# First hidden products in halves by head pair, tile 1's scores in one bank, another order of the first loads

## The chip, the core and the metric

The kernel runs on one core of a Trainium2 chip. The metric is the device time of one execution in microseconds (us); the kernel before takes 806.84 us (median of 3 runs, 805.37 to 808.19). The engines are PE (TensorE, matrix products; PEld is its weight load), ACT (ScalarE), DVE (VectorE), POOL (GpSimd) and SP (SyncE, which here only issues DMAs). Each runs its own instructions strictly in the order of its queue, and waits for the others by semaphores.

## The reference

Eight batches with eight heads of 576 tokens; the attention is local to chunks of 64 tokens, and its output (4608 tokens of 512 features) goes through a feed-forward block whose activation is h * cos(h).

```python
q_c, k_c, v_c = (a.reshape(B, H, S // 64, 64, D) for a in (q, k, v))
scores = (1.0 / np.sqrt(D)) * np.matmul(q_c, k_c.transpose(0, 1, 2, 4, 3))
scores = scores - np.max(scores, axis=-1, keepdims=True)
attn = np.exp(scores)
attn = attn / (np.sum(attn, axis=-1, keepdims=True) + 1e-09)
out = np.matmul(attn, v_c).reshape(B, H, S, D)
x = out.transpose(0, 2, 1, 3).reshape(B * S, H * D)       # 4608 x 512
h = x @ w_in                                              # w_in 512 x 2048
return (h * np.cos(h)) @ w_out                            # w_out 2048 x 512
```

The weights arrive as 64-bit floats, q, k and v as 32-bit ones.

## The kernel before

The 4608 tokens are nine tiles of 512. The work has two parts. In the first, tiles 0 and 1 (and the attention of tile 2) run while the weights arrive; each weight block (16 of `w_in`, 16 of `w_out`, 512 KB each) is turned from 64-bit bits into a float32 value and split into a high and a low part, so that a product of float32 accuracy is three fast matmuls: high by high, high by low, low by high (`hidden`, line 813; `split_weight`, line 504). In the second part the other tiles run in pairs with fewer products, from sums of weight blocks that the first part stored to HBM; its order is set by a planner of its own (`planned`), which the change does not touch.

The attention of tiles 0 and 1 (`early`, line 1138) goes by head pairs 0 to 3 (two heads side by side on the 128 partitions). For each pair: PE makes the scores (`scores_early`, 16 products of 64 x 64), DVE takes the maximum (L626) and subtracts it (L630), ACT exponentiates (L696), DVE sums (L712) and inverts (L716, L717), DVE or POOL multiplies by the inverse, called the quotient here (L481), PE transposes ("turns") the weights (L731), ACT copies them out (L477), PE multiplies by the values ("weighted"), and ACT and DVE split the result into the high and low part of x (L795, L798). Each pair's weighted result fills two PSUM banks, so four x splits make one half of x.

Weight blocks are read by two ACT instructions (`w`, L541, and `half`, L543), joined on DVE (L536), rounded to the high part on ACT or DVE (cast to `w_in` or `w_out`, L477 or L475), and the low part is the difference (L481 on POOL or DVE). `w` has two rooms, `half0` and `half1` one each.

A hidden block h(s) is 12 matmuls of 512 columns over the four pairs of x; the activation is six steps: ACT L831 rounds h/2pi, DVE L832 reduces, ACT L833 is the sine, which needs another function table than the exponential (so it comes behind all exponentials of tile 1), DVE L834 multiplies, which frees the PSUM bank of h, and the result is split (cast on ACT or DVE, `g_lo` on DVE or POOL). PSUM has eight banks: acc0 to acc3, two named h, and a0 and a1. h(0), h(1), h(3) and the later ones rotate over the two h banks; h(2) is in a1. So h(3) waits for L834 of h(0). The projection p(s), 12 matmuls of `g` and `w_out`, comes three hidden blocks later.

All of the first part is a list of pieces (`piece`, line 1046) with an engine, an assumed length and what each waits for. `placed` (line 162) puts them in an order by assumed times and by a due time from the table DUE, one number for each piece; `in_order` gives that order to the engines' queues. Pieces on PE that are longer than LONG go by due time, shorter ones as soon as they can.

Loads are issued by SP in one list. The first 22 issues (q and k of tile 0, `w_in` block 0, q and k of tile 1's pair 0, v of tile 0, `w_in` block 1, the other q and k of tile 1) come without a hold; behind them stand the remaining weight blocks. These are held by `touch` (line 1088), an instruction of one column on POOL that writes into the room of `w_in` block 2 and reads something that is ready late:

```python
raw, part = w_raw["in", 2][0].bitcast(F32)[:, :1], x_parts[0, 0][0][:, 0, :1].bitcast(F32)
two_by(POOL, raw, part, part, ALU.subtract)
```

Eight semaphores serve the loads in turn, so an issue also waits until the load eight places before it has landed.

Of the kernel before, what the change touches and what calls it, by code (L numbers as in the profile page):

```python
# [96 lines left out]
LONG = 2.0  # L97
# [33 lines left out]
    158.12, 58.9, 68.58, 63.65, 252.88, 143.8, 82.3, -250.55, 219.35, 114.51, -120.22, -295.86, 1e+09, -4.71,  # L131
# [5 lines left out]
    262.3, 48.25, 126.32, 193.62, 1e+09, 345.43, 23.97, -61.67, 75.14, -1.8, 433.58, 246.37, -62.79, 87.68, -8.61,  # L137
    -145.35, 32, 6.23, 84.32, 191.91, -66.13, 267.53, -107.91, 1e+09, 59.88, 1e+09, 1.78, 1e+09, 6.61, 1e+09,
    1e+09, -10.09, -254.05, 202.29, -15.1, 262.24, -166.36, 249.63, 71.08, 209.64, -226.64, 255.17, -18.33,
# [5 lines left out]
    -76.27, 1e+09, 292.24, -11.78, -101.18, 119.54, 173.07, 246.81, -59.42, 152.58, 59.6, 147.63, -111.18,  # L145
    -165.31, 170.18, 412.05, -234.16, 253.81, 56.94, 223.55, 174.74, 172.68, 262.87, 1e+09, -113.14, 133.26,
# [8 lines left out]
    199.71, 243.39, -154.74, 16.19, 1e+09, 1e+09, 143.88, -50.34, 1e+09, 1e+09, 1e+09, 1e+09, 1e+09, 1e+09,  # L155
    172.37, 92.61, 1e+09, 1e+09, 1e+09, 1e+09, 1e+09, 1e+09, 1e+09, 58.67, 248.55, 155.33, -25.97, 231.79, 141.91,
    1e+09, 1e+09, 153.74, 117.79, 119.81, 83.59, 470.08, 488.44, 258.14, 542.25, -17.83, 164.19, 314.55, 83.71,
    62.74, 350.71, -36.4, 242.13, -61.82, 228.28, 332.92, 1e+09, 437.5, 104.97, 27.99, 78.88, 1e+09, 458.39,
    -62.42, 304.54, 227.74, 1e+09, 424.55, 137.98, 50.14, 154.55, 190.64, 238.98, 240.92, 295.04, 313.65, -63.39,
    266.72, 327.78, 178.57, 212.45, 346.38, 151.22, 291.83, -2.81, 148.05, 154.34,  # L160
)


def placed(work, after_it, rank):

    n = len(work)
    left = [len(w[3]) for w in work]  # L170
# [266 lines left out]
def attention_then_cos_ffn(ctx: ExitStack, tc, qT, kT, v, w_in, w_out, out, wide):  # L437
# [630 lines left out]
    for hp in range(HP):  # L1068
        here["v", 0, hp] = loaded(0.25, load_v, 0, hp)
    here["in", 1] = loaded(0.5, load_weight, "in", 1)  # L1070
    for hp in range(1, HP):
        here["qk", 1, hp] = loaded(0.5, load_qk, 1, hp)
# [1386 lines left out]
```

## Time and profile before

| | us |
|---|---|
| median of 3 runs | 806.84 (805.37 to 808.19) |
| profiled execution, its own time | 804.86 |
| span of its instructions | 803.1 |
| PE busy | 789.8 (98%) |
| DVE, ACT, POOL busy | 691.7, 530.3, 204.0 |
| granted TensorE clock | 1.00 in all 40 slices |

The page's slices show PE busy at 9 tenths or more from the third slice on (a slice is 20 us), DVE likewise in most. Matmuls overlap one another, so a matmul's duration is longer than the step from one to the next; a row of 12 matmuls of one block takes about 2.72 us from its start to the start of what follows. Idle time in brackets is that of the engine just before the row, with what ended it.

### The profile page before, as it was taken

How to read it: one execution, taken by the hardware profiler on the slowest of the kernel's cores; microseconds unless marked ns; L12 is line 12 of the kernel's file. 1: busy time of each engine (PE TensorE's matmuls, PEld its weight loads, DVE VectorE, ACT ScalarE, POOL GpSimd, SP SyncE). 2: the span in 40 equal slices, each digit the busy share in tenths (PEclk: the TensorE clock that was granted, in tenths of full speed). 3: DMA queues.
4: the chain of work that ended last, by engine and by line, in shares of the span. 5: the costliest groups of instructions: out<-in, count | busy, mean ns of one | idle time of the engine just before them, and what ended most of it. 6: DMA issues, size and time to landing. Idle time of an engine off the chain costs nothing.

```text
span 803.1 us, 17487 instructions
## 1 busy us (share of the span) xinstructions
PE 789.8 (98%) x6720; PEld 698.8 (87%) x6720; DVE 691.7 (86%) x1071; ACT 530.3 (66%) x1006; POOL 204.0 (25%) x179
## 2 busy tenths in 40 slices
PE   5999999999999999999999999999999999999998
PEld 5788788888988898888999998888999988889998
DVE  6999998888888798999999988899999878789854
ACT  4988955455467766767777566889655566665552
POOL 2363765766812211410410001121001001000000
PEclk9999999999999999999999999999999999999999
DMA  8993739586988895987648779556665665556653
GB/s 315 388 417 140 263 131 317 182 309 200 281 301 245 315 311 197 305 285 245 205 154 268 236 222 323 204 196 199 222 215 185 194 222 189 183 184 211 211 184 105
DMA packets 95266, 189.88 MB, mean 236 GB/s; under 512 B 8656, under 2 KB 51664, under 8 KB 95184
## 3 DMA queue, kind: packets, MB, share of 16 engines
q1 hardware_dynamic: 95184, 188.78, 69.2%
q8 instruction: 53, 0.87, 0.4%
q14 instruction: 29, 0.24, 0.1%
HBM read 148.90 MB, written 39.85 MB: 235 GB/s over the span
## 4 chain that ended last, share of the span: by engine, by line
PE 90%; DMA 6%; DVE 2%; ACT 1%; issue 0%; SPq 0%; DVEq 0%
PE acc L471 55%; PE h L471 29%; PE a L471 5%; DMA w_out<-in_w_out_dram 5%; DMA kt<-in_kT_dram 1%; PE a L1585 1%; DMA qt<-in_qT_dram 1%; DVE w L536 1%; ACT g L833 0%; DVE g L832 0%; ACT w L541 0%; DVE w_in L481 0%; DVE g_lo L481 0%; DVE w_in L475 0%; DVE w_out L481 0%
## 5 line engine op out<-in xcount | busy, mean ns | idle before, releaser
L471 PE MATMUL h<-x,w_in 128*128 128x512 f32 (+1 forms) x852 | 190.6, 367 | 0.7 <-DVE g L834 0.7
L471 PEld LDWEIGHTS h<-x,w_in 128*128 128x128 f32 x852 | 147.8, 188 | 28.8 <-DVE g L834 1.4
L471 PE MATMUL acc<-w_in,w_in 128*128 128x512 f32 (+1 forms) x702 | 153.0, 346 | 0.0
L471 PEld LDWEIGHTS acc<-w_in,w_in 128*128 128x128 f32 x702 | 113.5, 188 | 16.6
L471 PE MATMUL acc<-w_out,g_hi 128*128 128x512 f32 x352 | 109.9, 393 | 0.3 <-DVE vt L475 0.3
L471 PE MATMUL acc<-w_in,g_hi 128*128 128x256 f32 x576 | 104.2, 282 | 0.0
L471 PEld LDWEIGHTS acc<-w_in,g_hi 128*128 128x128 f32 x576 | 88.3, 188 | 0.9
L471 PE MATMUL acc<-x,w_in 128*128 128x512 f32 x276 | 82.6, 392 | 0.0
L471 PE MATMUL acc<-w_in,g_lo 128*128 128x256 f32 x288 | 80.3, 279 | 0.0
L471 PEld LDWEIGHTS acc<-w_out,g_hi 128*128 128x128 f32 x352 | 64.2, 188 | 13.1 <-DVE vt L475 0.7
L471 PE MATMUL acc<-w_out,g_lo 128*128 128x512 f32 x176 | 68.7, 390 | 0.0
L1483 ACT ACTIVATE w_out<-w_out 128x512 f32<-128x512 f32 x96 | 60.1, 631 | 11.5 <-DVE w_out L1479 11.2
L481 DVE TENSOR_TENSOR g_lo<-w_out,g_hi 128x512 fp32r<-128x512 f32 x79 | 57.3, 730 | 10.8 <-ACT g_hi L477 9.1
L477 ACT CAST g_hi<-w_out 128x512 fp32r<-128x512 f32 x75 | 46.4, 620 | 28.2 <-PE acc L471 15.4
L471 PEld LDWEIGHTS acc<-x,w_in 128*128 128x128 f32 x276 | 51.6, 188 | 11.1
L471 PEld LDWEIGHTS acc<-w_in,g_lo 128*128 128x128 f32 x288 | 54.3, 189 | 0.0
L481 POOL TENSOR_TENSOR w_out<-g,w_out 128x512 f32<-128x512 f32 x10 | 14.2, 1422 | 143.1 <-ACT w_out L1483 143.1
L477 ACT CAST g_hi<-g 128x512 fp32r<-128x512 f32 x50 | 30.8, 623 | 25.6 <-DVE g L834 12.9
L481 POOL TENSOR_TENSOR g_lo<-w_out,g_hi 128x512 fp32r<-128x512 f32 x8 | 11.8, 1469 | 127.6 <-ACT g_hi L477 53.9
L471 PE MATMUL h<-w_in,g_hi 128*128 128x256 f32 x240 | 43.5, 282 | 0.0
L471 PEld LDWEIGHTS acc<-w_out,g_lo 128*128 128x128 f32 x176 | 33.0, 188 | 7.1
L1476 ACT ACTIVATE w_out<-g 128x512 int32<-128x512 f32 x48 | 29.9, 630 | 13.5 <-DVE g L1492 12.2
(216 smaller groups left out, 1687.0 us busy)
## 6 DMA issues: line engine op xcount, KB each, us to landing
w_in<-combo SPq DMA_DIRECT2D x112, 512.0 KB, 4.5
w_in<-sums SPq DMA_DIRECT2D x84, 512.0 KB, 3.5
combo<-w_in SPq DMA_DIRECT2D x56, 256.0 KB, 4.0
sums<-w_out SPq DMA_DIRECT2D x56, 256.0 KB, 4.5
qt<-in_qT_dram SPq DMA_DIRECT2D x36, 256.0 KB, 5.4
kt<-in_kT_dram SPq DMA_DIRECT2D x36, 256.0 KB, 5.4
w_in<-in_w_in_dram SPq DMA_DIRECT2D x16, 512.0 KB, 9.3
w_out<-in_w_out_dram SPq DMA_DIRECT2D x16, 512.0 KB, 9.9
```

Of the source, the lines that this page charges most:

```text
L471: kept(nc.tensor.matmul(*args, **kw))
L477: kept(nc.scalar.copy(out=out, in_=in_))
L481: kept(eng.tensor_tensor(out, a, b, op=op))
L536: kept(nc.vector.scalar_tensor_tensor(bits, bits, 3, low, op0=ALU.logical_shift_left, op1=ALU.bitwise_or))
L1476: kept(nc.scalar.activation(n.bitcast(I32), h, AF.Identity, bias=0.25, scale=0.5 / math.pi))
L1483: kept(nc.scalar.activation(g, g, AF.Sin, bias=0.5 * math.pi))
L1585: kept(nc.tensor.transpose(out=pt[:, i * P : (i + 1) * P], in_=e[:, 2 * i : 2 * i + 2].rearrange("p c k -> p (c k)"), identity=ident,))
```

## The change

The first two hidden blocks are made in halves: pairs 0 and 1 of h(0), then of h(1), then pairs 2 and 3 of both (HALVED, and `some` in `hidden`). LONG goes from 2.0 to 1.3, so that halves count as long pieces. Tile 1's scores all use bank a0, where they took a0 and a1 in turn; bank a1 takes the turned weights of tile 0's pairs 2 and 3, which used the two h banks. SP issues q and k of tile 1's pair 1 ahead of v of tile 0's pairs 2 and 3. `touch` reads tile 0's quotient of pair 3 (and waits for it), where it read the first x split. The assumed length of tile 1's weighted products is less, the assumed arrival of some loads later by 0.5, and the whole table DUE is another one (its rows are left out here).

```diff
-LONG = 2.0
+LONG = 1.3
+
+HALVED = 2
...
-        pt = ps_h.tile([P, 512], F32, name="h") if t == 0 else bank("a", hp)
+        pt = ps_h.tile([P, 512], F32, name="h") if t == 0 and hp < 2 else bank("a", hp if t else 1)
...
-    def hidden(t, fc):
-        h = bank("a", 1) if (t, fc) == order[2] else ps_h.tile([P, TOK], F32, name="h")
+    def hidden(t, fc, some=range(NCC), h=None):
+        if h is None:
+            h = bank("a", 1) if (t, fc) == order[2] else ps_h.tile([P, TOK], F32, name="h")
         w_hi, w_lo = w_parts["in", fc]
-        for cc in range(NCC):
+        for cc in some:
...
-    for hp in range(HP):
+    for hp in range(2):
+        here["v", 0, hp] = loaded(0.25, load_v, 0, hp)
+    arrival[0] += 0.5
+    here["qk", 1, 1] = loaded(0.5, load_qk, 1, 1)
+    for hp in range(2, HP):
         here["v", 0, hp] = loaded(0.25, load_v, 0, hp)
     here["in", 1] = loaded(0.5, load_weight, "in", 1)
-    for hp in range(1, HP):
+    arrival[0] += 0.5
+    for hp in range(2, HP):
         here["qk", 1, hp] = loaded(0.5, load_qk, 1, hp)
...
-        raw, part = w_raw["in", 2][0].bitcast(F32)[:, :1], x_parts[0, 0][0][:, 0, :1].bitcast(F32)
+        raw, part = w_raw["in", 2][0].bitcast(F32)[:, :1], weights_of(0, 1)[:, 1, 0, :1]
...
-            which = ("a", hp % 2) if t else ("acc", hp)
+            which = ("a", 0) if t else ("acc", hp)
...
+        if t == 0:
+            work[touch][3].append(q[3])
...
-            at = banks_free["a", hp % 2] if t else p.get(hp - 2)
+            at = banks_free["a", hp % 2] if t else banks_free.get(("a", 1)) if hp > 1 else None
...
+            elif hp > 1:
+                banks_free["a", 1] = banks_free["scored"] = p[hp]
...
-                PE, 0.9 * n if t else 0.8, made_by(key, lambda hps=hps, which=which: weighted(t, hps, [bank(*b) for b in which])),
+                PE, 0.6 * n if t else 0.8, made_by(key, lambda hps=hps, which=which: weighted(t, hps, [bank(*b) for b in which])),
...
-                if t == hp == i == 0:
-                    work[touch][3].append(hi)
...
+        if s < HALVED:
+            begun = piece(
+                PE, 1.36, made_by(("begun", s), hidden, t, fc, range(2)), begun, split["in", fc],
+                *x_done[t][:4], turned_out[0, 0],
+            )
+
+            def go(s=s, t=t, fc=fc, key=key):
+                made[key] = hidden(t, fc, range(2, NCC), made["begun", s])
+            stream = piece(PE, 1.36, go, stream, begun, *x_done[t])
```

What this does to the queues is seen at three places. On PE, from tile 1's second scores to the first hidden blocks, in the kernel before (`a0`, `a1` with `kt,qt` are scores of tile 1, `ident` marks a turn of tile 0's pairs 2 and 3, `x0` with `w_in0` is h(0)):

```order
L471 MATMUL a1_403<-kt_213,qt_212 64x64 x16
L731 MATMUL h_427<-ident_84,e1_282 128x128 x4
L731 MATMUL h_436<-ident_84,e1_282 128x128 x4
L471 MATMUL a0_483<-kt_217,qt_216 64x64 x16
...
L471 MATMUL a1_550<-kt_221,qt_220 64x64 x16
L471 MATMUL h_578<-x0_373,w_in0_441 128x512
...
L471 MATMUL h_578<-x0_524,w_in0_441 128x512
...
L471 MATMUL h_603<-x0_373,w_in1_591 128x512
```

The same stretch of PE now:

```order
L480 MATMUL a0_401<-kt_209,qt_208 64x64 x16
L740 MATMUL a1_464<-ident_84,e1_282 128x128 x4
L740 MATMUL a1_478<-ident_84,e1_282 128x128 x4
L480 MATMUL a0_487<-kt_217,qt_216 64x64 x16
...
L480 MATMUL a0_559<-kt_221,qt_220 64x64 x16
L480 MATMUL h_582<-x0_375,w_in0_508 128x512
...
L480 MATMUL h_596<-x0_375,w_in1_483 128x512
...
L480 MATMUL h_582<-x0_530,w_in0_508 128x512
```

The pieces stand in the same order; the banks differ, and the halves of h(0) and h(1) alternate behind tile 1's last scores.

On DVE, from the last inversion of tile 0 to tile 1's third subtraction, in the kernel before (L630 subtracts, L626 is the maximum, L481 the quotient, L536 joins a weight block, `w_308` being `w_in` block 0 and `w_380` block 1):

```order
L717 RECIPROCAL z_285<-z_285 128x16
L481 TENSOR_TENSOR e1_282<-e1_282,z_285 128x512
L630 TENSOR_TENSOR e0_332<-a0_315,m_333 128x512
...
L536 SCALAR_TENSOR_TENSOR w_308<-w_308,half0_89 128x512
...
L626 TENSOR_REDUCE m_420<-a1_403 128x8
L630 TENSOR_TENSOR e0_332<-a1_403,m_420 128x512
L626 TENSOR_REDUCE m_501<-a0_483 128x8
L536 SCALAR_TENSOR_TENSOR w_380<-w_380,half1_90 128x512
```

DVE there now (L639 subtracts, L635 is the maximum, L490 the quotient, L545 joins, `w_470` being block 1, L807 an x split, L721 a sum):

```order
L726 RECIPROCAL z_284<-z_284 128x16
L639 TENSOR_TENSOR e0_332<-a0_315,m_333 128x512
L490 TENSOR_TENSOR e1_282<-e1_282,z_284 128x512
...
L635 TENSOR_REDUCE m_418<-a0_401 128x8
L545 SCALAR_TENSOR_TENSOR w_470<-w_470,half1_90 128x512
L639 TENSOR_TENSOR e0_332<-a0_401,m_418 128x512
L545 SCALAR_TENSOR_TENSOR w_308<-w_308,half0_89 128x512
L807 TENSOR_TENSOR x0_376<-acc1_358,x0_375 128x4x64
L721 TENSOR_REDUCE z_510<-e0_332 128x8
L635 TENSOR_REDUCE m_505<-a0_487 128x8
L639 TENSOR_TENSOR e1_504<-a0_487,m_505 128x512
```

The subtraction of tile 1's pair 0 went ahead of the quotient, and both joins went between tile 1's second maximum and its third.

On ACT, from the last x splits of tile 0 to the first sine, in the kernel before (L543 and L541 read weight blocks, `w_in2_95`, `w_in3_97` and so on being blocks as they land, L795 an x split, L696 an exponential, L831 the first step of h(0)):

```order
L795 CAST x0_524<-acc2_529 128x4x64
L541 ACTIVATE w_572<-w_in2_95 128x512
L543 ACTIVATE half0_89<-w_in2_95 128x512
L477 CAST w_in1_591<-w_380 128x512
L543 ACTIVATE half1_90<-w_in3_97 128x512
L543 ACTIVATE half0_89<-w_out0_92 128x512
L696 ACTIVATE e1_500<-e1_500 128x512
L541 ACTIVATE w_601<-w_in3_97 128x512
L831 ACTIVATE g_618<-h_578 128x512
L696 ACTIVATE e1_500<-e1_500 128x512
L541 ACTIVATE w_626<-w_out0_92 128x512
L833 ACT_TABLE_LOAD
```

ACT there now (lines 9 or 10 higher):

```order
L552 ACTIVATE half1_90<-w_in3_97 128x512
L804 CAST x0_530<-acc2_536 128x4x64
L550 ACTIVATE w_579<-w_in2_95 128x512
...
L705 ACTIVATE e1_504<-e1_504 128x512
L552 ACTIVATE half0_89<-w_out0_92 128x512
L804 CAST x0_530<-acc3_537 128x4x64
L486 CAST w_in3_607<-w_589 128x512
L552 ACTIVATE half1_90<-w_in4_99 128x512
L550 ACTIVATE w_619<-w_out0_92 128x512
L841 ACTIVATE g_628<-h_582 128x512
...
L843 ACT_TABLE_LOAD
```

Two x splits of tile 0's pair 3 now stand behind the first reading of `w_in` block 3, and the first step of h(0) behind that of block 4, which in the kernel before came behind h(0)'s sine.

## Rows read from the trace of the kernel before

**Rows 1.** Busy time by stretches of the span, core 0 (engine busy, instruction count).

```profile
core 0: us, PE busy (x) PEld busy (x) DVE busy (x) ACT busy (x) POOL busy (x), PEclk, DMA share, GB/s
4.24:23.31 19.07, 14.81 (x401) 13.49 (x401) 15.29 (x30) 10.99 (x24) 5.04 (x5) 1.00 0.94 342
23.31:36.00 12.69, 11.97 (x54) 9.45 (x52) 11.72 (x20) 11.64 (x22) 4.09 (x3) 1.00 1.03 401
```

**Rows 2.** Waits of PE from 36 us to the end: total, times, longest.

```profile
PE acc L471 <- DVE vt L475: 0.3, 1, 0.3
```

**Rows 3.** Timeline of PE (start, duration, instruction): scores, weighted, turns, h(0).

```profile
4.28 1.97 PE L471 MATMUL acc<-kt,qt 64*64 64x64 f32 x32 [4.28 <-DMA kt<-in_kT_dram]
...
15.79 1.44 PE L471 MATMUL acc<-pts,vt 64*64 64x64 f32 x64
...
18.24 1.15 PE L471 MATMUL a<-kt,qt 64*64 64x64 f32 x32 [1.02 <-DMA kt<-in_kT_dram]
...
19.32 1.09 PE L731 MATMUL h<-ident,e 128*128 128x128 f32 x8
...
22.26 1.11 PE L471 MATMUL a<-kt,qt 64*64 64x64 f32 x32
...
23.31 5.80 PE L471 MATMUL h<-x,w_in 128*128 128x512 f32 x24
...
32.58 3.01 PE L471 MATMUL h<-x,w_in 128*128 128x512 f32 x12 [0.72 <-DVE g L834]
```

**Rows 4.** Timeline of DVE and ACT: instructions back to back.

```profile
13.53 1.23 ACT L696 ACTIVATE e<-e 128x512 f32<-128x512 f32 x2 [1.56 <-DVE e L630]
...
14.79 1.28 DVE L712 TENSOR_REDUCE z<-e 128x8 f32<-128x512 f32 x2
...
22.14 1.18 ACT L795 CAST x<-acc 128x256 fp32r<-128x256 f32 x4
...
22.75 1.41 DVE L798 TENSOR_TENSOR x<-acc,x 128x256 fp32r<-128x256 f32 x4
```

**Rows 5.** Timeline: quotients of tile 0, the touch, the first held load.

```profile
13.11 2.04 POOL L481 TENSOR_TENSOR e<-e,z 128x512 f32<-128x512 f32 x2 [11.80 <-DVE z L717]
...
16.60 0.69 DVE L481 TENSOR_TENSOR e<-e,z 128x512 f32<-128x512 f32 x1
16.71 1.48 POOL L481 TENSOR_TENSOR e<-e,z 128x512 f32<-128x512 f32 x1 [1.56 <-DVE z L717]
...
18.96 0.25 POOL L481 TENSOR_TENSOR w_in<-x 128x1 f32<-128x1 f32 x1 [0.77 <-ACT x L795]
...
19.23 0.33 SPq L468 DMA_DIRECT2D w_in<-in_w_in_dram  x1
```

**Rows 6.** Timeline: DVE beside POOL, two places.

```profile
32.87 1.30 POOL L481 TENSOR_TENSOR w_out<-w,w_out 128x512 fp32r<-128x512 f32 x1 [4.63 <-ACT w_out L477]
...
33.63 1.09 DVE L481 TENSOR_TENSOR g_lo<-g,g_hi 128x512 fp32r<-128x512 f32 x1
...
37.20 1.36 POOL L481 TENSOR_TENSOR g_lo<-g,g_hi 128x512 fp32r<-128x512 f32 x1 [3.03 <-ACT g_hi L477]
...
37.33 1.27 DVE L716 TENSOR_SCALAR z<-z 128x16 f32<-128x16 f32 x1
```

**Rows 7.** Timeline: landings of `w_in` blocks 1, 3 and 4.

```profile
16.77 0.68 ACT L541 ACTIVATE w<-w_in 128x512 f32<-128x512 f32 x1 [0.29 <-DMA w_in<-in_w_in_dram]
...
25.97 0.67 ACT L543 ACTIVATE half<-w_in 128x512 uint32<-128x512 uint32 x1 [1.02 <-DMA w_in<-in_w_in_dram]
...
30.89 0.33 SPq L468 DMA_DIRECT2D w_in<-in_w_in_dram  x1
```

**Rows 8.** Timeline: from the first step of h(0) to the release of its bank.

```profile
29.87 1.28 ACT L833 ACT_TABLE_LOAD   x1
...
31.83 0.69 DVE L834 TENSOR_TENSOR g<-h,g 128x512 f32<-128x512 f32 x1
```

**Rows 9.** Timeline of PE: h(5).

```profile
44.43 2.99 PE L471 MATMUL h<-x,w_in 128*128 128x512 f32 x12
```

More of the change, by code (lines that the diff above doesn't have):

```diff
@@ L112 @@
 DUE = (
[18 rows of a table removed]
-    158.12, 58.9, 68.58, 63.65, 252.88, 143.8, 82.3, -250.55, 219.35, 114.51, -120.22, -295.86, 1e+09, -4.71,
[5 rows of a table removed]
-    262.3, 48.25, 126.32, 193.62, 1e+09, 345.43, 23.97, -61.67, 75.14, -1.8, 433.58, 246.37, -62.79, 87.68, -8.61,
-    -145.35, 32, 6.23, 84.32, 191.91, -66.13, 267.53, -107.91, 1e+09, 59.88, 1e+09, 1.78, 1e+09, 6.61, 1e+09,
-    1e+09, -10.09, -254.05, 202.29, -15.1, 262.24, -166.36, 249.63, 71.08, 209.64, -226.64, 255.17, -18.33,
[5 rows of a table removed]
-    -76.27, 1e+09, 292.24, -11.78, -101.18, 119.54, 173.07, 246.81, -59.42, 152.58, 59.6, 147.63, -111.18,
-    -165.31, 170.18, 412.05, -234.16, 253.81, 56.94, 223.55, 174.74, 172.68, 262.87, 1e+09, -113.14, 133.26,
[8 rows of a table removed]
[L155 to L160, printed above, removed]
[55 rows of a table added]
 )
@@ L1153, in early @@
             banks_free[which] = piece(DVE, 0.6, rest_of(key, 1), m, room)
-            if t and which == ("a", 1):
-                banks_free["scored"] = banks_free[which]
             e[hp] = piece(ACT, 0.6, lambda hp=hp: exponentials_early(t, hp), banks_free[which], table=AF.Exp)
@@ L1259, in attend_third @@
         return w
-    stream = None
+    stream = begun = None
     held = {}
@@ L1274, in attention_then_cos_ffn @@
         bank_at = held.get(s - (3 if s < 5 else 2)) if s > 2 else None
-        stream = piece(
-            PE, 2.72, made_by(key, hidden, t, fc), stream, split["in", fc], bank_at,
-            *x_done[t], *([turned_out[0, 1]] if s < 2 else ()), *([banks_free["scored"]] if s == 2 else ()),
-        )
+        if s < HALVED:
[6 more added lines that the diff above has]
+            stream = piece(PE, 1.36, go, stream, begun, *x_done[t])
+        else:
+            stream = piece(
+                PE, 2.72, made_by(key, hidden, t, fc), stream, split["in", fc], bank_at,
+                *x_done[t], *([banks_free["scored"]] if s == 2 else ()),
+            )
         hid = stream
```

91 rows, old and new, of the table DUE are left out of this document.

## The prediction

> **What bounds the kernel now.** I read the busy time by stretches first. From 4.24 to 23.31 us PE is busy 14.81 of 19.07; from 23.31, where h(0) begins, to 36 it is 11.97 of 12.69 [rows 1]. The waits of PE from there to the end are one of 0.3 [rows 2]. So PE is the bound from 23.31 on, nothing behind 36 us can be won but that 0.3, and the end moves by as much as PE's products move in the opening. The question is when h(0) begins, and what PE waits for between h(0) and h(5), which now begins at 44.43 [rows 9].
>
> Second, the timeline of PE up to h(3). Tile 0's pairs 0 and 1 are weighted by 17.23; tile 1's second scores come at 18.24, held by the landing of their keys; the fourth scores start at 22.26 and h(0) 1.05 later. 24 products then run in 5.80; h(3) starts at 32.58 after a wait of 0.72 for L834 [rows 3].
>
> Third, the timelines of DVE and ACT, for the price of one step in a full queue: two sums in 1.28 with 0.68 each, so 0.60 from start to start on DVE; two exponentials in 1.23, taken as 0.55 to 0.60 on ACT; four x splits in 1.18 on ACT (0.26) and in 1.41 on DVE (0.33) [rows 4]. All times below are those steps laid end to end in the new order, each at the later of its queue and its input (some 0.04 to hand over).
>
> **The change part by part.** No product goes or comes: h(0) is 12 matmuls in halves as well as whole. LONG, the assumed lengths and DUE act by the order alone.
>
> *Keys of pair 1 earlier.* They now stand ahead of `w_in` block 1, so they land before its 16.75 [rows 7]. The second scores then wait for weighted pair 1 (17.23 [rows 3]) and for bank a0, that is for the subtraction of tile 1's pair 0. This is moved ahead of the quotient on DVE, so it takes the quotient's 16.60 [rows 5] and ends at 17.2. Second scores 17.25 to 18.4: 1.0 earlier. That is all that this edit gives.
>
> *The quotient behind it, and the touch.* In the kernel before DVE's quotient started at 16.60 and POOL's at 16.71; POOL's took 1.48 where two took 2.04 before, 1.02 each [rows 5]. So the second to start waited for the first. Elsewhere it is DVE that waits: `g_lo` beside POOL's 32.87 to 34.17 takes 1.09 and ends 0.55 behind it, a scalar step beside POOL's 37.20 to 38.56 takes 1.27 [rows 6]. Now DVE is at the subtraction, whose input is in PSUM, when POOL starts; POOL's quotient runs 16.7 to 17.75, and DVE's, due at 17.1, ends 0.55 behind it, at 18.3 instead of 17.29. The touch waits for that one: 18.35 to 18.6, and the held loads start at 18.65 instead of 19.23 [rows 5], 0.55 to 0.6 earlier. They could land as much earlier and not more: `w_in` block 3 at 25.4 (25.95 now) and block 4 at 30.3 (30.88 now) [rows 7].
>
> The Trainium skill says the same in "SBUF — State Buffer", section "Who interferes with whom": a VectorE instruction with both inputs in SBUF and a GpSimd one that reads SBUF lock each other out for the whole instruction, and the order of issue decides who waits. The trace agrees, with 1.48 against 1.02. Without that rule the quotient would end at 17.8, and the sum below would be about 1.0 less.
>
> *One bank for tile 1's scores.* Each pair's scores now wait for the subtraction of the pair before, on DVE. Its queue from 18.3: three x splits to 19.3, second maximum to 19.95, the join of `w_in` block 1, second subtraction 20.45 to 21.15. (Block 1 lands 1.3 later than now, as the keys stand ahead of it: 18.05 instead of 16.75 [rows 7]; ACT reads it from 18.3, behind its splits, until 19.5, so the join's input is there.) Third scores 21.2 to 22.3. Then DVE: join of block 0 from 21.05, a split, a sum, third maximum 22.6, third subtraction 23.3 to 24.0. Fourth scores 24.0; h(0) 1.05 behind [rows 3], at **25.1** instead of 23.31: 1.8 later. PE's other pieces stand beside this: the turns of pairs 2 and 3 end at 21.0 and the weighted ones at 23.7. Block 0's low part, on POOL behind block 1's, is there at 24.2.
>
> *The halves.* They begin only behind the fourth scores, so they fill no gap ahead of h(0). They give x of pair 3 until 28.5, 1.36 more. But x of pair 3 now stands behind `w_in` block 3's first reading on ACT. Pair 3 is weighted at 23.7, ACT waits until 25.4, and its last cast comes after two more readings, an exponential and another reading: 25.4 + 3.45 = 28.85, the low part at 29.3. h(0)'s last three products lose some 0.8; h(0) is done at 29.8, h(1) at 31.15, h(2) at 33.9.
>
> *h(3) and the bank of h(0).* On ACT the first step of h(0) stands behind the reading of block 4 (landing 30.3): two readings of 0.55, then this step at 31.45, the last exponential, the cast of `w_out` block 0 (32.6), the table load at 33.15 (29.87 now, 1.28 long [rows 8]), the sine to 35.1. DVE would then free the bank; but it is at tile 1's inversion, whose scalar step starts at 33.5 beside POOL's low part of `w_out` block 0 (33.25 to 34.55) and is held as in [rows 6]; the quotient follows, and L834's step runs 35.65 to 36.35. So h(3) starts at **36.4** instead of 32.58: 3.8 later.
>
> *To h(5).* Behind h(3) stand p(0), h(4), p(1): 4 blocks of 2.72 and one turn of 0.6, where the kernel before has two (the other now falls into the wait ahead of h(3)). 36.4 + 10.9 + 0.6 = 47.9 against 44.43 [rows 9]: 3.45 later. h(4)'s bank (40.1) and weights (41.1) are there for 41.9. From there the other engines do at 47.9 what they did at 44 to 47, so they have more room than before, and PE runs on; the one wait of 0.3 [rows 2] probably goes.
>
> Costed at nothing: the stores of blocks in another order and the moved work of tile 1 and 2's attention, since PE waits for none of these behind 36 us [rows 2] and now comes later still; up to 0.5 if a stage behind is tight, 0.3 the other way.
>
> Sum: 3.45 − 0.25 = **3.2 later**. The profiled execution takes 804.86 for a span of 803.1; it would take 808.1. The median shown is 806.84, so I forecast **810.0**. Bounds: without the two locks 1.0 less; with both landings another 1.0 earlier, 1.0 less, though not below h(3) at 34.9, as the fourth subtraction and the table load then set it: +1.7. With the hold no earlier and a landing 1.0 later: +4.7. The steps themselves may be off by 0.3. So 808.5 to 811.5 if the mechanism is right.
>
> **Rivals.** *The landings don't bind (not slower).* If blocks 3 and 4 landed by 24.1 and 27.4, ACT would not stop; h(0) would still start at 25.1, but h(3) at 33.7, h(5) 0.8 later than now: 807.6. For it: ACT's order is made for earlier landings than the trace shows. Against it: they need to come 1.8 and 3.5 us earlier than now, the hold is released 0.6 earlier, and the load queue moves at 401 GB/s with a DMA share of 1.03 in that stretch [rows 1].
>
> *The opening shrinks as meant (faster).* Decided by the fourth scores: if DVE gave the third subtraction by 21.8, h(0) could begin at 22.85, which is also the floor: behind 17.23 PE still has three scores, two turns and two weighted pairs, 3 × 1.05 + 1.1 + 1.44 = 5.7 [rows 3]. With that, the wait of 0.72 and the 0.3 gone: 0.45 + 0.72 + 0.3 = 1.5, 805.3; together with the tenths beside PE's waits no more than 2. Against it: DVE's twelve steps between 17.2 and 24.0 leave no gap but the quotient's wait.
>
> *The clock (slower still).* PE gets a pause of nearly 2 us ahead of h(3). The granted clock is 1.00 in both stretches [rows 1], pauses of 1.2 included, but the first 32 score products took 1.97 where 32 later ones take 1.15 [rows 3]. If h(3) and p(0) ran at that ratio of 1.7, two blocks of 2.72 would take 3.8 more: 813.8. Nothing in the granted clock speaks for it.
>
> **How the numbers follow.** Forecast 0.76, no binding landings 0.13, faster opening 0.06, clock 0.05. A measurement here tells 0.3% (2.4 us) from no change: faster is below 804.4, slower above 809.3. Of the forecast's own range four fifths lie above 809.3 (0.60), the rest within; with the clock 0.64. The second case is within but for 0.01, the third about half below 804.4 with the runs' own spread. I give 0.63 slower, 0.32 within, 0.05 faster. The range is 807.0 to 812.0: it takes in the second case's 807.6 and leaves out the other two and the forecast's ends.
>
> **What would show it.** Tile 1's scores at about 17.25, 21.2 and 24.0; h(0) near 25.1; an idle of ACT of over 1 us ahead of a reading of `w_in`, with an x cast right behind it; the touch at 18.4; DVE's quotient over 1 us long; the table load near 33.2; PE idle for 2 us ahead of h(3), ended by L844; no wait of PE behind 50 us. It would be wrong if h(0) began before 23.3, or if h(3) followed h(2) at once.

## The result, and the profile after

The changed kernel takes 810.77 us (median of 6 runs, 808.52 to 812.47) beside 807.32 for the kernel before on the same chip: a ratio of 1.0051, 95% interval 1.0036 to 1.0066. It is slower, as forecast (810.0, range 807 to 812). The loss is 3.5 us by these medians and 4.1 by the ratio. Over all its later runs, on four chips, the kernel before has a median of 806.52 (94 runs, 804.84 to 809.52). The profiled execution took 811.88 for a span of 810.1, 7.0 more than that of the kernel before. Here line numbers are 9 to 10 higher (L834 is now L844).

Busy time by stretches, to h(0) and from there to the end of h(3) (answers to [rows 1]):

```profile
core 0: us, PE busy (x) PEld busy (x) DVE busy (x) ACT busy (x) POOL busy (x), PEclk, DMA share, GB/s
4.24:25.43 21.19, 16.98 (x401) 15.28 (x401) 16.99 (x32) 11.64 (x23) 6.14 (x6) 1.00 0.95 339
25.43:41.10 15.67, 12.58 (x56) 9.56 (x54) 11.88 (x21) 12.53 (x23) 5.61 (x4) 1.00 1.03 410
```

PE's waits behind 41 us: total, times, longest (to [rows 2]):

```profile
PE h L480 <- DVE g L844: 1.7, 2, 1.3
```

PE has the same 401 instructions ahead of h(0), 2.12 us later, then idles 3.09 of 15.67 us where it idled 0.72 of 12.69. The wait of 0.3 of [rows 2] is gone, and two of another kind have come far behind the opening.

PE's timeline after (start, duration, instruction, in brackets the wait ahead), to [rows 3] and [rows 9]:

```profile
17.47 1.09 PE L480 MATMUL a<-kt,qt 64*64 64x64 f32 x31
...
20.47 0.66 PE L740 MATMUL a<-ident,e 128*128 128x128 f32 x4 [1.32 <-ACT pts L486]
21.38 1.08 PE L480 MATMUL a<-kt,qt 64*64 64x64 f32 x29 [0.25 <-DVE e L639]
...
24.35 1.15 PE L480 MATMUL a<-kt,qt 64*64 64x64 f32 x32 [0.54 <-PE acc L480]
25.43 3.70 PE L480 MATMUL h<-x,w_in 128*128 128x512 f32 x15
30.35 2.58 PE L480 MATMUL h<-x,w_in 128*128 128x512 f32 x9 [1.22 <-ACT x L804]
...
37.52 0.63 PE L740 MATMUL a<-ident,e 128*128 128x128 f32 x4 [1.87 <-DVE e L490]
38.02 3.02 PE L480 MATMUL h<-x,w_in 128*128 128x512 f32 x12
...
49.53 2.65 PE L480 MATMUL h<-x,w_in 128*128 128x512 f32 x11
```

Second, third and fourth scores come at 17.47, 21.38 and 24.35 (forecast 17.25, 21.2, 24.0), h(0) at 25.43 (25.1). The turn of pair 3 waits 1.32 for ACT's copy of pair 2, since bank a1 now takes the turned weights of both pairs. But this wait does not set the third scores: behind the turn they wait another 0.25, for DVE's second subtraction. The fourth scores wait 0.54 for the third one; the view names PE's weighted products, which had ended by 23.81. Both subtractions, on DVE:

```profile
20.65 0.68 DVE L639 TENSOR_TENSOR e<-a,m 128x512 f32<-128x512 f32 x1
...
23.55 0.69 DVE L639 TENSOR_TENSOR e<-a,m 128x512 f32<-128x512 f32 x1
```

They end at 21.33 and 24.24, and the scores start 0.05 and 0.11 later: the single bank sets both, as forecast. h(3) comes at 38.02 (36.4), h(5) at 49.53 (47.9). With 44.43 in [rows 9], the opening is 5.10 later in this pair of profiles, and from h(5) to the end it takes 760.57 instead of 758.67: 1.90 more, where I had written nothing.

The quotients, the touch and the held loads (to [rows 5]), then ACT and DVE up to the release of h(0)'s bank (to [rows 7, 8]):

```profile
16.72 0.63 DVE L639 TENSOR_TENSOR e<-a,m 128x512 f32<-128x512 f32 x1
17.26 1.27 DVE L490 TENSOR_TENSOR e<-e,z 128x512 f32<-128x512 f32 x1
...
16.94 1.04 POOL L490 TENSOR_TENSOR e<-e,z 128x512 f32<-128x512 f32 x1 [1.50 <-DVE z L726]
18.68 0.20 POOL L490 TENSOR_TENSOR w_in<-e 128x1 f32<-128x1 f32 x1 [0.69 <-ACT x L804]
...
18.90 0.33 SPq L477 DMA_DIRECT2D w_in<-in_w_in_dram  x1
19.27 1.50 SPq L477 DMA_DIRECT2D w_out<-in_w_out_dram  x1
20.82 0.43 SPq L477 DMA_DIRECT2D w_in<-in_w_in_dram  x1
...
26.91 0.67 ACT L552 ACTIVATE half<-w_in 128x512 uint32<-128x512 uint32 x1 [2.73 <-DMA w_in<-in_w_in_dram]
27.49 0.35 ACT L804 CAST x<-acc 128x256 fp32r<-128x256 f32 x1
...
29.94 0.36 ACT L804 CAST x<-acc 128x256 fp32r<-128x256 f32 x1
...
32.24 0.67 ACT L552 ACTIVATE half<-w_in 128x512 uint32<-128x512 uint32 x1 [1.40 <-DMA w_in<-in_w_in_dram]
...
33.37 0.57 ACT L841 ACTIVATE g<-h 128x512 int32<-128x512 f32 x1
...
34.99 1.28 ACT L843 ACT_TABLE_LOAD   x1
...
35.41 0.94 DVE L725 TENSOR_SCALAR z<-z 128x16 f32<-128x16 f32 x1
...
37.29 0.68 DVE L844 TENSOR_TENSOR g<-h,g 128x512 f32<-128x512 f32 x1
```

DVE's quotient is held by POOL's, as forecast (1.27, end 18.53). The first held load is issued at 18.90 instead of 19.23. But the second issue took 1.50 on SP, where it took 0.54 before, and the third, block 3's, came at 20.82 instead of 20.19. Block 3 lands at 26.9, not 25.4, and block 4 at 32.2, not 30.3. ACT stands 2.73 for the one, with both x casts of pair 3 behind it, and 1.40 for the other, with h(0)'s first step behind it.

The two late waits begin on SP's queue (after), then DVE and PE:

```profile
176.13 3.21 SPq L930 DMA_DIRECT2D combo<-w_in  x4
181.03 0.33 SPq L477 DMA_DIRECT2D w_in<-combo  x1
181.48 0.36 SPq L900 DMA_DIRECT2D out_dram<-pts  x1
...
183.16 1.06 SPq L900 DMA_DIRECT2D out_dram<-vt  x2
...
185.67 0.69 DVE L1021 TENSOR_TENSOR pts<-e 128x512 f32<-128x512 f32 x1 [2.56 <-DMA out_dram<-pts]
189.69 0.69 DVE L1021 TENSOR_TENSOR vt<-e,e 128x512 f32<-128x512 f32 x1 [3.33 <-DMA out_dram<-vt]
190.30 0.68 DVE L844 TENSOR_TENSOR g<-h,g 128x512 f32<-128x512 f32 x1
...
191.04 3.00 PE L480 MATMUL h<-x,w_in 128*128 128x512 f32 x12 [1.26 <-DVE g L844]
```

In the kernel before, SP issues tile 1's output row stores first:

```profile
174.24 0.34 SPq L890 DMA_DIRECT2D out_dram<-vt  x1
174.73 1.45 SPq L890 DMA_DIRECT2D out_dram<-pts  x2
176.30 0.38 SPq L890 DMA_DIRECT2D out_dram<-vt  x1
176.91 3.10 SPq L920 DMA_DIRECT2D combo<-w_in  x4
```

After, four kept sums and a load behind them go first, a second load stands between the stores, and vt's stores go last. The stores read the rooms pts and vt, and DVE's differences of tile 2 (L1021) need those rooms: DVE stands 3.33 for the landing of a store, L844 stands behind it, and PE waits for L844.

### The profile page after: what moved, and what is told of

Same layout as the page of the kernel before. It is cut to its first block, busy times and chain, and to the rows that moved or that the text cites. A ratio compares the mean times of both kernels' runs of the same rounds, so it can differ in the third digit from the quotient of the medians.

```text
span 810.1 us, 17478 instructions
## 1 busy us (share of the span) xinstructions
PE 793.1 (98%) x6720; PEld 700.5 (86%) x6720; DVE 687.6 (85%) x1066; ACT 531.6 (66%) x1009; POOL 208.2 (26%) x181
## 4 chain that ended last, share of the span: by engine, by line
PE 92%; DVE 4%; DMA 3%; ACT 1%; issue 1%; SPq 0%; ACTq 0%; DVEq 0%
PE acc L480 56%; PE h L480 30%; PE a L480 5%; DMA w_in<-in_w_in_dram 1%; PE a L1610 1%; DMA out_dram<-vt 1%; DMA kt<-in_kT_dram 1%; DVE w_in L1031 0%; DVE e L639 0%; DVE z L721 0%; DVE m L635 0%; DVE g L842 0%; DVE w_in L490 0%; DVE x L1031 0%; PE a L740 0%
## 5 line engine op out<-in xcount | busy, mean ns | idle before, releaser
L490 DVE TENSOR_TENSOR g_lo<-w_out,g_hi 128x512 fp32r<-128x512 f32 x79 | 57.2, 729 | 10.8 <-ACT g_hi L486 9.1
L490 POOL TENSOR_TENSOR w_out<-g,w_out 128x512 f32<-128x512 f32 x10 | 14.2, 1423 | 143.1 <-ACT w_out L1508 143.1
L490 POOL TENSOR_TENSOR g_lo<-w_out,g_hi 128x512 fp32r<-128x512 f32 x8 | 11.7, 1467 | 127.6 <-ACT g_hi L486 53.9
```

What stands on the lines that cost most here:

```text
L490: kept(eng.tensor_tensor(out, a, b, op=op))
```

## The experiments

The edits move finished pieces in the planned list right before they are issued; `move(a, b)` puts piece a right behind b. The moves are shown in words and only the main ones; pieces that hang on a moved one were moved with it. Experiments 7 and 8 also change the order of the loads, experiment 6 changes nothing. Ratios are to the kernel before, with 95% intervals; the changed kernel is at 1.0051.

**1. Kept sums behind the stores.**

```diff
+move(kept sums 4, last store of tile 1's output rows)
```

> The changed kernel, with the four transfers that keep tile 1's first sums (combo<-w_in, pieces of keep_sums 4) put behind tile 1's output row stores on SyncE's queue, as in the kernel before; nothing else moves. Theory A (the stores' place makes the late waits by itself): the waits of PE at 191.0 (1.43) and 202.7 (0.64) us, both ended by L844 behind L1021, go; the stores are issued some 5 to 7 us earlier; the span falls by 2.07, so about 0.997 of the changed kernel's time, some 808.7 where that is 810.8. Rival B (the late waits are carried over from the late opening): they stay at 1.4 and 0.6, and the time stays at 810.8.

808.23 us, 1.0020 (1.0008 to 1.0032). SP issues the stores at 178.63 to 181.26, the waits of L844 are gone, and from h(5) (49.38) to the end of the span (807.7) it takes 758.3. Theory A: these waits come from the place of the stores. By the ratios they cost 2.5 us.

**2. The same order, alone, in the kernel before.**

```diff
+move(kept sums 4, last load of tile 2's keys)
```

> The kernel before, with the same four transfers put ahead of tile 1's output row stores (the one place where the late order differs, made alone). Theory A: two waits of PE ended by L834 appear behind 180 us and cost 1.5 to 2.1; the time is 0.2 to 0.26% above the kernel before, 808.8 to 809.4. Rival B: without the late opening there is slack, no wait appears, ratio 1.000.

807.10 us, 1.0007 (0.9997 to 1.0017): nearer to rival B. The stores come at 177.76 to 180.76, behind the four sums, but the two loads that follow the sums stayed behind the stores. DVE stands 4.28 there for the landing of a store of pts, at 179.29 to 183.57, and yet PE does not wait for L834. So the sums alone don't do it; experiment 1 took sums and loads out of the way. In the changed kernel a load stands ahead of the stores, vt's stores come last (here the first of them comes first), and DVE waits twice. Its opening is later too, and with the stores in the same place the late waits of PE shrink as the opening comes earlier: 1.7 in the changed kernel, 1.5 in experiment 3 and 0.8 in experiment 4 (both below), with h(5) at 49.53, 48.27 and 46.59. Which of these spares the kernel before was not tested.

**3 and 4. ACT's readings of blocks that have not landed.** Experiment 3 moves block 4's alone, experiment 4 that and block 3's with what hangs on it:

```diff
+move(lower in 4, sine of h(0))
 # experiment 4 besides:
+move(x pair 3 first, a cast of x pair 2);  move(x pair 3 second, x pair 3 first)
+move(lower in 3, lower out 0);        move(upper in 3, lower in 3)
+move(join in 3, subtraction of tile 1 pair 3)
```

> The changed kernel, with ACT's first reading of w_in block 4 (L552) moved from ahead of h(0)'s first step (L841) to behind its sine (L843). Theory A (the reading of a block that has not landed holds h(0)'s first step, and so the bank of h(3)): the table load starts near 33 instead of 35.0 and h(3) near 36 instead of 38.0; the time falls by 1.5 to 2.0, to 808.8 to 809.3. Rival B (h(0)'s own late end, by the x casts, sets it): h(0) ends at 31.9 as it does now, so h(3) comes no more than 0.7 earlier, and the time stays within 0.1%. Rival C (SyncE's long issue and the landing are of the profiled execution alone, in most runs the block is there): no change in the time, and in the profile h(3) is at 36 in both.

> The changed kernel, with ACT's and DVE's readings of the held blocks back behind what PE waits for: both casts of x of pair 3 ahead of w_in block 3's readings, w_in block 4's first reading behind h(0)'s sine. Theory A: h(0)'s waits of 1.39 and 0.23 (ended by the x casts, L804) go, h(0) still begins near 25.4, h(3) comes at 33.7 to 34.3 instead of 38.0; the late waits of 2.07 stay; the time falls by up to 4, to 807 to 808. Rival B (the blocks' landing itself is what binds, since h(3) reads block 3): h(3) stays behind 36 us and less than 1 is won. Rival C (the profiled execution of the changed kernel had a late landing that most runs don't have): h(3) at 34 in the profile, but the time falls by only 1 to 2.

Experiment 3: 809.83 us, 1.0040 (1.0028 to 1.0053); h(3) at 36.79. The saving is 0.9, half of what theory A asked, and not clear of the noise; h(0)'s wait for the x casts (1.25), rival B's reason, is still there. Experiment 4: 808.45 us, 1.0028 (1.0018 to 1.0038). Its PE timeline:

```profile
25.40 5.75 PE L480 MATMUL h<-x,w_in 128*128 128x512 f32 x24
...
34.57 0.63 PE L740 MATMUL a<-ident,e 128*128 128x128 f32 x4 [0.67 <-DVE e L490]
35.08 3.01 PE L480 MATMUL h<-x,w_in 128*128 128x512 f32 x12
```

24 products run through, the waits for x are gone, and h(3) comes 2.94 earlier. The time falls by only 1.9, as rival C said. Rival C's reason is not borne out as it stands: block 3 landed 8.0 to 8.5 behind the first held issue in all three profiles with this opening (the changed kernel, experiments 1 and 3). It is experiment 4's profile that is a quick one, with 6.9; it took 807.47, beside a median of 808.45.

**5. Both edits.**

> The changed kernel with both earlier edits together: casts of x of pair 3 ahead of w_in block 3's readings, block 4's first reading behind h(0)'s sine, and tile 1's kept sums behind its output row stores. Theory A (the two costs are independent): the late waits of L844 behind 180 us are gone, h(3) stays near 35, h(5) near 46.6 (2.1 behind the kernel before); the time is 0.8 to 1.2 below that of the run with the readings alone (its late waits were 0.52 and 0.60), 0.14 to 0.18% above the kernel before. Rival B (the stores no longer matter once the opening is earlier, as in the kernel before with the same edit): the same time as with the readings alone, 0.28% above.

806.79 us, 1.0001 (0.9992 to 1.0011): the two costs add, and together they are the loss, as far as the interval tells. The time is 2.2 below experiment 4 by the ratios, where theory A had 0.8 to 1.2 from the late waits of that profile. h(0) stands at 24.87, h(5) at 46.03, and still it is level with the kernel before. So the first profile of the kernel before (h(5) at 44.43) may not be the usual one; experiment 6 asks that.

**6. A second profile of the kernel before**, nothing changed.

> The kernel before, unchanged, for a second profile of it. Theory A (the profiled execution of before was a quick one: 804.86 where the runs have a median of 806.5, because w_in block 3 landed early for it, at 25.95, and ACT's readings and the table load stand behind that landing): block 3 lands at 26.5 to 28, h(3) is 0.5 to 2 later than 32.58, and the span is longer by the same amount. Rival B (the scatter lies elsewhere): h(5) at 44.4 to 44.7 again, and the span differs from 803.1 by waits behind 50 us.

806.91 us, span 805.1. PE's timeline:

```profile
18.84 1.15 PE L471 MATMUL a<-kt,qt 64*64 64x64 f32 x32 [1.97 <-DMA kt<-in_kT_dram]
...
21.82 1.76 PE L471 MATMUL a<-kt,qt 64*64 64x64 f32 x30
...
25.47 5.82 PE L471 MATMUL h<-x,w_in 128*128 128x512 f32 x24
...
34.55 3.02 PE L471 MATMUL h<-x,w_in 128*128 128x512 f32 x12 [0.54 <-DVE g L834]
...
46.37 3.00 PE L471 MATMUL h<-x,w_in 128*128 128x512 f32 x12
```

Two stretches of it by engine; the third number from the end is the granted clock:

```profile
18.84:20.00 1.16, 1.16 (x33) 1.09 (x34) 1.16 (x3) 1.02 (x4) 0.30 (x1) 0.96 0.30 99
20.00:23.40 3.40, 3.40 (x40) 3.07 (x42) 1.70 (x4) 2.39 (x5) 1.27 (x1) 0.51 0.69 211
```

h(0) and h(5) are 2.16 and 1.94 later than in [rows 3, 9], from two causes: the wait for the second keys is 1.97 instead of 1.02, and behind it PE runs at half clock for 3.4 us. Block 3 lands at 27.9 (theory A), but that only keeps the loss; it starts earlier than I expected. Against this profile the changed kernel's opening is 3.16 later and its rest 1.84. Two more profiles have the old opening, the same up to h(0): experiment 2's, with a wait of 1.37 for the keys, h(5) at 44.69 and the clock at 1.00, and experiment 12's, with 1.81, h(5) at 47.01 and half clock for as long as here. So the first profile is one of two kinds, and neither is an exception.

**7. The keys alone, in the kernel before** (an edit of the order in which loads are issued), with ACT's readings of block 1 behind its copies; **8. the same, and the table load right behind h(0)'s first step.**

```diff
-v0 v1 v2 v3, w_in 1, keys 1, keys 2, keys 3
+v0 v1, keys 1, v2 v3, w_in 1, keys 2, keys 3
+move(upper in 1, copy of pair 3);  move(lower in 1, upper in 1)
 # experiment 8 besides:
+move(last exponential of tile 1, its subtraction);  move(upper out 0, sine of h(0))
```

> The kernel before with tile 1's second keys loaded ahead of tile 0's last values (two banks for the scores, whole h and the hold as before), and ACT's readings of w_in block 1, which now lands later, behind its copies of pairs 2 and 3. Theory A (the wait for the keys, 1.2 ahead of the second scores, is the one thing that this part removes, and nothing else is late): second scores at 17.3 instead of 18.24, h(0) at 22.4 to 22.8 instead of 23.31, but h(3) is set by the exponential, the table load and L834 behind it, so it gains only 0.3 to 0.6; the time is 0.04 to 0.08% below the kernel before. Rival B: the later block 1 takes it back, h(0) at 23.3 or later, ratio 1.000 or above.

> As the run with the keys alone, and besides ACT's last exponential of tile 1 ahead of h(0)'s first step and the upper reading of w_out block 0 behind the sine, so that the table load follows the first step at once. Theory A: the wait ahead of h(3) (0.89 in the kernel before) goes to 0.2 or less, h(3) at 31.0 to 31.6 instead of 32.58, h(5) 0.8 to 1.4 earlier; the time is 0.10 to 0.17% below the kernel before, a version that beats both. Rival B: w_out block 0's low part (34.17 in the kernel before) comes later and p(0) waits for it, so that only 0.3 stays, ratio 0.9995 or above.

806.37 us, 1.0000 (0.9987 to 1.0013), and 806.07, 0.9996 (0.9985 to 1.0008). With the keys alone the second scores come at 17.01 and h(0) at 22.96, 0.35 earlier than in [rows 3], but PE then waits 1.22 for L834 ahead of h(3) instead of 0.72: nothing is left. In experiment 8 the profile shows what hangs on block 3's landing, with ACT's row first:

```profile
27.65 0.67 ACT L543 ACTIVATE half<-w_in 128x512 uint32<-128x512 uint32 x1 [2.51 <-DMA w_in<-in_w_in_dram]
...
34.83 4.62 PE L471 MATMUL h<-x,w_in 128*128 128x512 f32 x12 [2.91 <-DVE g L834]
```

ACT stands 2.51 for block 3, PE 2.91 for L834, and then h(3) takes 4.62 at half clock.

**9. The opening reordered** around the single bank, with both edits of experiment 5; **10 and 11**: besides, the steps ahead of h(3), and then those behind it.

```diff
+move(copy of pair 2, its turn);  move(lower in 1, copy of pair 3);  move(upper in 1, lower in 1)
+move(maximum of tile 1 pair 1, its scores);  move(subtraction, maximum);  move(join in 0, quotient)
 # besides, in 9 to 11: h(0) whole ahead of h(1)
 # 10: join, inversion and quotient of tile 1 behind L844; table load right behind L841
 # 11: g_hi, g_lo and block 4 ahead of that quotient; turns of tile 1 behind h(4)
```

> As the run with both edits, and besides the opening reordered on ACT, DVE, POOL and PE with the one bank for tile 1's scores kept: block 1's two readings on ACT behind the copies of pairs 2 and 3 (L486), tile 1's second maximum and subtraction ahead of the x splits and of block 1's join on DVE, block 0 joined right behind the quotient, h(0) run whole ahead of h(1). Theory A (h(0) is late because ACT's copy of pair 2 waits behind a block that lands 1.3 later, and because joins and splits stand ahead of the second subtraction; the one bank as such costs little): the turn of pair 3 comes at 19.6 to 20.0 instead of 20.2 to 20.9, third scores near 20.3, fourth near 22.9, h(0) at 23.2 to 24.0 instead of 25.4; the time is 1.4 to 2.2 below the run with both edits, level with the kernel before or 0.1% below. Rival B (the one bank itself is the chain: scores, maximum, subtraction, scores): third scores not before 20.8, fourth not before 23.7, h(0) not before 24.8, less than 0.7 won.

> As the run with both edits and the opening reordered, and besides, ahead of h(3): tile 1's last maximum and subtraction ahead of the joins, its last exponential and block 3's readings ahead of h(0)'s first step, the table load right behind that step, w_out block 0's readings behind the sine, tile 1's inversion and quotient behind L844, and the first turn of tile 1 behind p(0). Theory A (h(3) is held by what stands ahead of L844 on ACT and DVE, not by the landings): h(0) at 23.5 to 24.2, h(3) at 32.0 to 32.8 instead of 34.95, h(5) near 44.0 to 44.6; the time is 0.15 to 0.27% below the kernel before, a version that beats both. Rival B: w_out block 0, now read later, holds p(0) by 1 us or more, so that the time is level with the kernel before (0.9995 to 1.0005).

> As e_best, with the steps behind L844 put right: h(0)'s g_hi and g_lo (L484, L490 on DVE) straight behind L844 instead of behind the quotient of tile 1, h(1)'s first step and sine and the readings and casts of w_in block 4 ahead of that quotient, the turns of tile 1 behind h(4). Theory A (the waits of e_best, 2.02 ahead of p(0) ended by g_hi and 1.40 and 0.79 ahead of h(4) ended by block 4's cast, all come from g_hi's place behind the quotient): all three go, h(0) to h(5) takes 20.2 to 20.6 where the kernel before takes 20.9 to 21.1, with h(0) at 23.8 to 24.8; the time is 0.10 to 0.25% below the kernel before and below the changed kernel by 0.6 to 0.75%. Rival B: the quotient, now later, holds tile 1's turns and weighted pairs, or p(1) waits for w_out block 1, by 1 us or more, and the time is level with the kernel before or above.

Experiment 9: 807.06 us, 1.0002 (0.9993 to 1.0011). The wait ahead of the turn of pair 3 falls from 1.83 (experiment 5) to 0.73, h(0) comes at 24.11, but 1.87 is lost again ahead of h(3), by DVE's quotient of tile 1: theory A for the opening, and nothing in the time. With two banks and early keys (experiment 7) h(0) came at 22.96; what the single bank still costs was not tested alone. Experiment 10: 810.72, 1.0047 (1.0031 to 1.0063); experiment 11: 808.27, 1.0017 (1.0008 to 1.0026). PE's waits in 10, then in 11:

```profile
33.91 2.91 PE L480 MATMUL h<-x,w_in 128*128 128x512 f32 x12
38.66 0.70 PE L480 MATMUL acc<-w_out,g_hi 128*128 128x512 f32 x2 [1.85 <-DVE g_hi L484]
...
45.08 0.74 PE L480 MATMUL h<-x,w_in 128*128 128x512 f32 x2 [1.19 <-ACT w_in L486]
46.43 3.78 PE L480 MATMUL h<-x,w_in 128*128 128x512 f32 x9 [0.62 <-POOL w_in L490]
```

```profile
32.54 2.90 PE L480 MATMUL h<-x,w_in 128*128 128x512 f32 x12
...
47.08 3.31 PE L480 MATMUL h<-x,w_in 128*128 128x512 f32 x7 [2.53 <-DVE g L844]
```

In both h(3) starts without a wait, and what I moved behind it is late next: g_hi behind the quotient in 10; in 11 h(3)'s first step, behind ACT's copy of a turn that I had put behind h(4). Both theories A fall. Rival B has the time of 11, but not the wait; in 10 neither fits: p(0) waits for g_hi and not for `w_out` block 0, and the time is far above level.

**12. The kernel before, with more room ahead of block 3's readings.**

```diff
+move(lower in 3, exponential of tile 1 pair 2);  move(upper in 3, lower in 3)
+move(upper out 0, sine of h(0))
```

> The kernel before with three ACT readings in another order: w_in block 3's two behind w_out block 0's first reading and an exponential of tile 1, w_out block 0's second behind h(0)'s sine. Theory A (what binds ahead of h(3) is the chain landing of block 3, readings, first step, exponential, table load, L834): h(3) at 31.5 to 32.2 instead of 32.58, and less scatter from run to run, since the landing has 1.2 us of room; the median is 0.10 to 0.18% below the kernel before. Rival B: w_out block 0 comes later by as much and p(0) waits, ratio 0.9995 or above.

806.08 us beside 807.23, 0.9988 (0.9980 to 0.9997): 0.6% below the changed kernel by the ratios, and below the kernel before by an interval that just leaves out 1, the only one of these versions to do so. Block 3 landed at 28.9 in its profile, and ACT did not stand for it. But h(3) came at 35.19 behind a wait of 0.80 for L834, where theory A had 31.5 to 32.2, and h(0) to h(3) took 9.33, beside 9.27 in [rows 3]: the time fits theory A, its mechanism is not shown.

## Why the prediction was right, and where it was not

The sum (3.2 later) came close to the measured 3.5 to 4.1; its parts did not, and that they add up so well is luck. The stores, costed at nothing, took more than half of the loss, and of the 3.45 in the opening ACT's readings account for 1.5 to 1.9.

*Right, by the profile.* Second scores, DVE's quotient behind POOL's, the subtractions and scores of the single bank, and h(0) are all within 0.35 of their times. On the quotient the trace agrees with the Trainium skill, "SBUF — State Buffer", section "Who interferes with whom": of a VectorE instruction with both inputs in SBUF and a GpSimd one that reads SBUF, the one that is issued second waits for the whole of the other. It was POOL's, 1.48, in [rows 5]; now it is DVE's, 1.27 beside POOL's 1.04. The scalar step beside POOL's low part of w_out block 0 was held too, as forecast (0.94, against 0.17 for the same step at 16.34). The shape of the rest was right too: an x cast behind a block's reading, h(0)'s first step behind another, a pause ahead of h(3).

*Failed: "They could land as much earlier and not more".* I took the landing as the first held issue plus 6.7, as in the one profile I had. Over the 14 profiles of this case block 3 lands 6.7 to 8.7 behind that issue, 8.0 in the changed kernel's: the hold won 0.33, and the landing scatters by 2.0. The scatter goes with the issues ahead of it on SP: in the five profiles whose first three held issues took 0.33 to 0.54 each, block 3 landed 6.7 to 6.9 behind the first, and in the five whose second one took 1.18 to 1.50, 8.0 to 8.7. With block 4 late by 1.9, this is where the 1.6 come from by which h(3) came later than forecast.

*Failed: "Costed at nothing: the stores of blocks in another order".* I had cleared this by [rows 2]: PE waits for none of these stores there. But [rows 2] were taken where the stores go first, and say nothing of them in another place. Behind the sums and a load they cost 1.8 to 1.9 in the profile and 2.2 to 2.5 by the ratios of experiments 1 and 5, more than half of the whole loss.

*Mis-sized: the opening.* I had 3.45 to h(5). Undoing the readings gives back 1.5 to 1.9 (experiments 4 and 5 against the runs without), and with the stores undone too the ratio is 1.0001, at most 1.0011, although the single bank, the halves and the lock are all still there. So most of h(0)'s 1.8 was a loss against the profile I read: the kernel before itself waits up to 1.97 for its keys in other executions and then runs at half clock (experiment 6, and 12 with the same opening). Some of it may remain: of the runs with a mean clock of 0.999 or more, 9 of experiment 5 have a median of 806.70, and 26 of the kernel before on the same chip one of 805.89. A forecast against one profiled execution carries that execution's luck: 804.86, beside a median of 806.52.

*The rivals.* Block 3's and block 4's landings bind, so the case without them (807.6) is out. The faster opening is out: in no version did h(0) begin ahead of 22.85, and in none with the single bank ahead of 24.11. The clock, to which I gave 0.05 because no row spoke for it, is there, but in the kernel before as well, and it does not separate the two: the changed kernel's profile keeps 1.00 behind the 1.87 ahead of h(3), and its two runs with a mean clock of 0.999 or more took 811.88 and 810.75.

*Open.* Which part of the late order makes the stores costly (the loads, the order of the four stores, or the later opening), what lengthens an issue on SP, and how much the single bank costs at full clock. Whether two banks for the scores and whole h would beat the one bank with the edits of experiment 5 was not tried alone, nor was the hold by itself.

## What to carry to other kernels

A new order is read on every queue to its end, the transfer queue first: a store that has moved behind a load that waits holds its room, and the engine that wants the room holds all that is queued behind it, 140 us away from the edit. It costs time only where that engine has no room left: in experiment 2 DVE stood 4.28, and PE did not wait. In an in-order queue, a reading of something that is still in flight belongs behind everything that is ready and wanted; here that won 1.5 to 1.9 us. And before a forecast of half a per cent, ask how usual the one profiled execution is.

## What the runs showed of the hardware

TensorE's granted clock fell from 1.00 (2.4 GHz) to 0.50 (1.2 GHz) for 3 to 4 us in six of the 14 profiles, soon after PE had waited: 1.97 us in experiment 6, 1.8 to 2.9 in the others, with up to 1.5 us at 1.00 in between (in experiment 11 still within the wait; in experiment 10 a second time, behind waits of 1.19 and 0.62). Waits of 1.83, 1.87 (twice), 1.89 and 2.03 in other profiles were followed by no fall. Of the 94 runs of the kernel before, the 63 with a mean clock of 0.999 or more have a median of 805.92, the other 31 one of 807.48: this and the landings are what I found of the scatter of a kernel's runs.

In 13 of the 14 profiles at least one of the loads issued ahead of 30 us (four in experiment 12) took 0.8 to 1.5 us to issue on SP, where most take 0.33 to 0.5. In seven it was the second held one (1.50 in the changed kernel), otherwise another (the fourth held one in experiment 4, 1.36), and the landings behind it shifted. What makes it so long stays open.
